# An MLP kernel in which the normalised rows of two token blocks are transposed by VectorE and placed by DMAs instead of by TensorE through PSUM

## The chip, the cores and the metric

One core of one Trainium2 chip. The metric is the device time of one execution in microseconds, the median of several runs. All numbers are of float32 data (TensorE works on float32 and on float32 split into a rounded part and a remainder).

## The reference, cut to what matters

A transformer block with adaptive normalisation, on 2048 tokens of width 576. An attention part (32 heads, one shared key and value head) is followed by an MLP of inner width 4608. What the change touches is the input of the MLP:

```python
h = _layernorm(x) * (1 + cb) + sb
y = _layernorm(h)
h = _gelu(y @ w1 + b1)
x = x + gb * (h @ w2 + b2)
```

For the product with `w1` the rows of `y` (token by feature) must lie transposed, with features on the partitions.

## The kernel before

**Tiling.** The 2048 tokens are four blocks of 512 (`NB`, `TB`), each of four tiles of 128 tokens (`NT`). The MLP takes the blocks in two pairs: the first pass handles blocks 0 and 1, the second blocks 2 and 3. In each pass there are 18 rounds (`NG`), one for each group of 256 inner features; so `v` counts 36 rounds, 0 to 35. Both matrix products use a scheme with seven products in place of eight (`A11`, `S2`, `S3`, `A12`, `S1`, `A22`, `S4`), for which sums of blocks of the operand are formed beforehand.

**A round.** The loop (from L1359) emits for each of the seven products the product with `w1` (`product`, L1156), the load of the same weights for the next round (`load_w1`, L792, on SyncE's queue), work of VectorE and ScalarE on the result (`gelu`, L1159 to L1177), and one step of the second matrix product of the round before (`fc2s`, L1247; its matmuls are L1259). Each step of `fc2s` uses both buffers of the PSUM tile `psA` (two tiles), and VectorE empties them in L1265. A step cannot start before VectorE has emptied the buffers of the step before. Each step then has its own weights for the next round loaded (`load_w2s`, L1223, SyncE's queue). The operands of `fc2s` are sums that GpSimd makes (`sums`, L1225 to L1245, with L1232 and L1233).

The step of `fc2s` between the two halves of product `S2` (the hook `mid`, L1397) is the seventh of the step list; the one right after `S2` is the first of the next list. They are called the seventh step and the first step below.

**Slots.** After each of the seven products the loop calls `more` (L1366). These seven calls of a round are called slots 1 to 7 here. In rounds 1 to 16 a slot advances the generator `ln2_pair` (L701) by one step, and this generator prepares the normalised rows of blocks 2 and 3, tile by tile, beside the MLP of blocks 0 and 1. Where the coming step contains a transposition it is marked `"T"`, and then only slots 3 and 4 (`room=True`) may run it; in round 16 (`NG - 2`) any slot may. In round 17 (`NG - 1`) whatever is left of the generator is run at once, and `op_pieces` (L1051) begins to form the operands of the second pass from `YR[1]`.

**The stages of a tile** are numbered steps (`ln2_stages`, L658). Stage 0 takes the statistics of the row on VectorE (L143, L670, L671), stage 1 turns them into scale and bias on GpSimd (L675 to L677), stage 4 normalises on ScalarE into a tile `Z` (L683), stage 5 applies scale and shift on GpSimd (L686, L687), stages 8 and 9 repeat the statistics and scale for the result, and stage 12 normalises again on ScalarE (L690, L691) and adds a bias row on GpSimd (L692). Stages 14 and 15 transpose: four and one TensorE transpositions of 128 by 128 into a PSUM tile (L155), each followed by a ScalarE copy into `yr` (L165). Tile i's stage k is put at step 10 i + k:

```python
return {0: lambda: stats(0), 1: lambda: scale(0), 4: norm, 5: rows, 8: lambda: stats(1), 9: lambda: scale(1),
        12: renorm, 14: lambda: turn(0, 4, ac), 15: lambda: turn(4, 5, ac)}
```

After the eighth tile the generator has two operations of GpSimd on `YR[1]`, one after the other (L714, L716); their result is what the operand `T2` of the second pass is copied from. In round 17, slot 2 forms `T2` (ScalarE L1069, named `+T2`), slot 3 its remainder (`-T2`, VectorE L1071) and the difference `=T3` (VectorE L1062), and only then comes the step of the second matrix product `fc2` (L1282; matmuls L1293, emptied by VectorE L1330), which uses the two `psA` buffers as well.

**The buffers.** `Z` is the tile `Z2`, with two buffers that are taken in turn. After the last tile the same two buffers receive weights (`load_w2`, L1135 to L1141).

**Queues.** Every engine works through its instructions in the order in which the program emits them. All DMAs of this part are issued by SyncE, in that order; one that has to wait holds up those behind it.

Of the kernel before, what the change touches and what calls it, by code (L numbers as in the profile page):

```python
# [8 lines left out]
F32 = mybir.dt.float32  # L9
# [9 lines left out]
KD = 5  # L19
# [13 lines left out]
def block_kernel(ctx: ExitStack, tc, x, wqkv, wo, w1, b1, w2, b2, c, wmod, ident_in, out):  # L33
    nc = tc.nc
    ve, ac, po, pe, sy = nc.vector, nc.scalar, nc.gpsimd, nc.tensor, nc.sync
# [17 lines left out]
    def psB(): return PS["t"].tile([128, 512], F32, name="psB", bufs=PS["b"])  # L53
# [27 lines left out]
    at = tc.tile_pool(name="at", bufs=1, side="right")  # L81
# [59 lines left out]
    def ln_stats1(src):  # L141
        stt = per.tile([128, 2, 6], F32, name="bst", bufs=3)
        ve.bn_stats(stt[:, 0, :], src[:, :288])  # L143
        return stt
# [9 lines left out]
    def tr(o, Z, k):  # L154
        pe.transpose(o, Z[:, 128 * k:128 * (k + 1)], ident)  # L155

    def transpose_tile(Z, yr, t, k0, k1, e):
        p = psB()
        for k in range(k0, k1):
            tr(p[:, 128 * (k - k0):128 * (k - k0 + 1)], Z, k)  # L160
        n = k1 - k0
        src = p[:, :128 * n].rearrange("p (k c) -> p k c", k=n)
        dst = yr[:, k0:k1, 128 * t:128 * (t + 1)]
        if e is ac:
            ac.activation(dst, src, AF.Copy)  # L165
        else:
            ve.tensor_copy(dst, src)
# [286 lines left out]
    for tb in range(NB):  # L454
        nz = big() if tb + 1 < NB else None
        for i, m in enumerate((4, 0, 1, 2, 3)):
# [27 lines left out]
            if tb < 2:  # L484
                for _ in range(NSTAT[tb][i]):
                    ln1_stats(*stats.popleft())
                for _ in range(NAPPLY[tb][i]):
                    b, t = applies.popleft()
# [8 lines left out]
    px = pxp.__enter__()  # L497
# [160 lines left out]
    def ln2_stages(tb, t):  # L658

        X = XT[:, NT * tb + t, :]  # L660
        o = {}

        def small(n):
            return per.tile([128, n], F32, name="sm2", bufs=8)

        def stats(i):
            src = o["h"] if i else X
            o["mv", i] = small(2)
            stt = ln_stats1(src)
            ve.bn_stats(stt[:, 1, :], src[:, 288:])  # L670
            ve.bn_aggr(o["mv", i], stt)  # L671

        def scale(i):
            mv, rs, nb = o["mv", i], small(1), small(1)
            po.tensor_scalar(rs, mv[:, 1:2], EPS, None, op0=ALU.add)  # L675
            po.tensor_tensor(rs, rs, nhalf, op=ALU.pow)
            po.tensor_scalar(nb, mv[:, 0:1], rs, -1.0, op0=ALU.mult, op1=ALU.mult)  # L677
            o["sc", i] = dict(scale=rs, bias=nb)

        def norm():  # L680
            Z = o["Z"] = px.tile([128, 640], F32, name="Z2", bufs=2)
            o["h"] = Z[:, :D]
            ac.activation(o["h"], X, AF.Identity, **o["sc", 0])  # L683

        def rows():
            po.tensor_mul(o["h"], o["h"], BC[:, 1, :])  # L686
            po.tensor_tensor(o["h"], o["h"], BC[:, 0, :], op=ALU.add)  # L687

        def renorm():
            ac.activation(o["Z"][:, D:], o["Z"][:, 512:D], AF.Identity, **o["sc", 1])  # L690
            ac.activation(o["h"], o["h"], AF.Identity, **o["sc", 1])  # L691
            po.tensor_tensor(X, X, B2["b"], op=ALU.add)  # L692

        def turn(k0, k1, e):
            yr = YR[tb // 2][:, KD * (tb % 2):KD * (tb % 2 + 1)]
            transpose_tile(o["Z"], yr, t, k0, k1, e)

        return {0: lambda: stats(0), 1: lambda: scale(0), 4: norm, 5: rows, 8: lambda: stats(1), 9: lambda: scale(1),
                12: renorm, 14: lambda: turn(0, 4, ac), 15: lambda: turn(4, 5, ac)}

    def ln2_pair():  # L701
        YR[1] = per.tile([128, 2 * KD, TB], F32, name="yr", tag="big", bufs=3)
        at = {}
        for _ in range(2):
            yield
        for i in range(2 * NT):
            for k, f in ln2_stages(2 + i // NT, i % NT).items():
                at.setdefault(10 * i + k, []).append((k >= 14, f))
        for k in range(max(at) + 1):
            for _, f in at.get(k, ()):  # L710
                f()
            yield "T" if any(t for t, _ in at.get(k + 1, ())) else None
        R = YR[1]
        po.tensor_tensor(R[:, 5:7], R[:, 7:9], R[:, 5:7], op=ALU.subtract)  # L714
        yield
        po.tensor_tensor(R[:, 5:7], R[:, 5:7], R[:, 0:2], op=ALU.add)  # L716
        yield
# [274 lines left out]
    for n in range(NQT):  # L992
# [8 lines left out]
        for tok in order:  # L1001
            if tok[0] == "V":
                g = int(tok[1:])
                while g:
                    i = min(g, 4 - pq % 4)
# [16 lines left out]
            elif tok == "WP":  # L1022
                h2 = part.popleft()
                p = psB()
# [81 lines left out]
    px = ctx.enter_context(tc.tile_pool(name="mx", bufs=1, side="right", reuse_waits="tile"))  # L1106
# [175 lines left out]
    def fc2(v):  # L1282
# [22 lines left out]
        for bt in range(2 * NT):  # L1305
# [30 lines left out]
            yield  # L1336

    fill = deque([ln2_pair()])
    f2 = deque()
    gens, sm = deque(), deque()  # L1340
# [175 lines left out]
```

## Time and profile before

| | |
|---|---|
| runs | 2221.74, 2223.95, 2224.66 us; median 2223.95 us |
| the profiled execution | 2222.87 us, of which 2221.0 us are the span from the first to the last instruction |
| busy in the span | TensorE 99%, its weight loads 65%, VectorE 87%, ScalarE 74%, GpSimd 69% |
| DMA | 307.71 MB in 184632 packets, mean 139 GB/s |
| granted TensorE clock | 0.999 of full speed over the span |
| the first pass of the MLP, rounds 0 to 17 | from 1388.0 to 1793.7 us of the span |

A row of a timeline gives the start (us from the span's start), the duration in us, the engine, the line of the kernel, the operation, what it writes and reads, the shape and how many are merged in the row; in brackets, the idle time of the engine just before and what ended it. PE is TensorE, PEld its weight loads, DVE VectorE, ACT ScalarE, POOL GpSimd, SPq the queue of SyncE.

### The profile page before, as it was taken

Reading aid. Unit: us, or ns where it says so; the run is one execution under the profiler, and the core shown is the slowest. Engines: PE = TensorE matmul, PEld = TensorE weight load, DVE = VectorE, ACT = ScalarE, POOL = GpSimd, SP = SyncE. Lnnn points to the kernel's source line nnn. Section 1 sums busy time; section 2 is a strip of 40 time slices with the busy share of each in tenths; the row PEclk is TensorE's granted clock in tenths of the full one; section 3 lists DMA queues with packets and bytes.
Section 4 is the critical chain, followed back from the end, with each engine's and each line's share of the span. In section 5 each row is a group of like instructions: output and inputs, shape, how many; then the busy total and the mean of one; then the engine's idle time right before and its main releaser. Section 6 shows DMA issues by size and latency. Waiting matters only on the chain.

```text
span 2221.0 us, 46122 instructions
## 1 busy us (share of the span) xinstructions
PE 2201.4 (99%) x16643; PEld 1449.3 (65%) x16643; DVE 1932.7 (87%) x3415; ACT 1639.2 (74%) x3144; POOL 1526.4 (69%) x1762
## 2 busy tenths in 40 slices
PE   8999999999999999999999999999999999999999
PEld 5654444444544545444454446888888899889898
DVE  7689999999999999999999983888888878788887
ACT  5569999999999999999999998544445444343443
POOL 7654455666776687678676540888888867877776
PEclk9999999999999999999999999999999999999999
DMA  6242143443333332333333321666666646676663
GB/s 228 86 133 92 34 134 117 135 129 116 126 119 118 115 130 97 112 130 111 117 127 117 120 70 63 207 178 175 179 179 180 184 128 182 180 219 189 178 183 123
DMA packets 184632, 307.71 MB, mean 139 GB/s; under 512 B 19695, under 2 KB 75391, under 8 KB 184405
## 3 DMA queue, kind: packets, MB, share of 16 engines
q1 hardware_dynamic: 184261, 304.62, 43.9%
q8 instruction: 132, 2.16, 0.4%
q14 instruction: 95, 0.78, 0.1%
q10 hardware_dynamic: 144, 0.15, 0.0%
HBM read 200.68 MB, written 93.79 MB: 133 GB/s over the span
## 4 chain that ended last, share of the span: by engine, by line
PE 93%; DVE 1%; ACT 1%; issue 0%; ACTq 0%; DVEq 0%
PE psC L932 24%; PE psB L1156 18%; PE psA L1259 16%; PE psB L942 14%; PE psM L319 13%; PE psB L731 2%; PE psB L952 2%; PE psA L1293 1%; PE psA L731 1%; PE psB L155 0%; PE psB L248 0%; PE psB L357 0%; PE psM L942 0%; ACT P L944 0%; DVE mx L344 0%; DVE gs L1168 0%
## 5 line engine op out<-in xcount | busy, mean ns | idle before, releaser
L944 ACT ACTIVATE P<-psB 128x512 f32<-128x512 f32 x2013 | 1054.4, 619 | 42.3 <-PE psM L319 20.6
L964 DVE TENSOR_REDUCE mx<-psM 128x1 f32<-128x512 f32 x1476 | 934.3, 682 | 28.5 <-PE psM L319 15.6
L942 PE MATMUL psB<-qst,KS 64*128 64x512 f32 x2013 | 605.1, 433 | 0.1
L319 PE MATMUL psM<-KS,qst 64*128 64x512 f32 x1722 | 590.2, 434 | 0.7 <-DVE mx L337 0.2
L932 PE MATMUL psC<-P,V 128*32 128x256 f32 (+3 forms) x6608 | 568.1, 439 | 0.0
L942 PEld LDWEIGHTS psB<-qst,KS 64*128 64x128 f32 x2013 | 301.7, 184 | 218.6 <-ACT P L944 186.2
L319 PEld LDWEIGHTS psM<-KS,qst 64*128 64x128 f32 x1722 | 283.5, 184 | 185.6 <-DVE mx L964 130.3
L1156 PE MATMUL psB<-ops,w1a 128*128 128x512 f32 x1512 | 393.9, 396 | 0.2 <-DVE h L1171 0.2
L1156 PEld LDWEIGHTS psB<-ops,w1a 128*128 128x128 f32 x1512 | 270.1, 188 | 46.7 <-DVE h L1171 0.6
L932 PEld LDWEIGHTS psC<-P,V 128*32 128x32 f32 x6608 | 147.0, 108 | 187.7 <-issue 160.2
L1265 DVE TENSOR_TENSOR XT<-psA,XT 128x576 f32<-128x576 f32 x330 | 241.8, 753 | 18.6 <-PE psA L1259 13.2
L1259 PEld LDWEIGHTS psA<-w2s,big 128*128 128x128 f32 x1584 | 223.0, 188 | 14.0 <-POOL big L1233 2.5
L1259 PE MATMUL psA<-w2s,big 128*128 128x288 f32 x1584 | 230.5, 294 | 0.0
L1169 ACT ACTIVATE psB<-gs 128x512 f32<-128x512 f32 x144 | 86.7, 602 | 127.6 <-DVE gs L1168 127.4
L1233 POOL TENSOR_TENSOR big<-s,big 128x512 fp32r<-128x512 f32 x132 | 171.0, 1295 | 10.6
L962 DVE CUSTOM_DVE_ANT_0 xc<-psM,xc 128x512 f32<-128x512 f32 x246 | 166.3, 682 | 12.9 <-PE psM L319 4.4
L1165 ACT ACTIVATE h<-psB,b1t 128x512 f32<-128x512 f32 x144 | 98.1, 681 | 100.7 <-PE psB L1156 76.7
L768 POOL TENSOR_TENSOR os<-O,os 128x512 fp32r<-128x512 f32 x31 | 39.8, 1285 | 171.8 <-ACT os L767 171.8
L955 ACT ACTIVATE xc<-psB 128x512 f32<-128x512 f32 x246 | 154.1, 626 | 3.0 <-PE psM L319 0.2
L1168 DVE SCALAR_TENSOR_TENSOR gs<-psB,h 128x512 f32<-128x512 f32 x144 | 98.6, 684 | 38.5 <-ACT psB L1166 38.4
L802 POOL TENSOR_TENSOR r<-r,r 128x256 fp32r<-128x256 f32 (+1 forms) x162 | 121.8, 752 | 13.0
L1174 ACT ACTIVATE big<-h 128x512 fp32r<-128x512 f32 x39 | 24.7, 634 | 133.8 <-DVE h L1171 133.8
(217 smaller groups left out, 3327.5 us busy)
## 6 DMA issues: line engine op xcount, KB each, us to landing
w1a<-w1scr SPq DMA_DIRECT2D x252, 256.0 KB
w2s<-w2sum SPq DMA_DIRECT2D x132, 288.0 KB
w1scr<-r SPq DMA_DIRECT2D x126, 256.0 KB
w2s<-w2scr SPq DMA_DIRECT2D x76, 288.0 KB
w2scr<-r SPq DMA_DIRECT2D x72, 288.0 KB
w2sum<-r SPq DMA_DIRECT2D x72, 288.0 KB
qst<-qscr SPq DMA_DIRECT2D x192, 72.0 KB
w1a<-w2scr SPq DMA_DIRECT2D x33, 288.0 KB
```

Source lines behind the costliest of these rows:

```text
L319: pe.matmul(o, QST[n][64 * g:64 * g + 64, p, 128 * qt:128 * (qt + 1)], KS[64 * g:64 * g + 64, 512 * kb:512 * (kb + 1)], start=True, stop=True)
L802: po.tensor_tensor(o[:, n:2 * n], src, o[:, :n].bitcast(F32), op=ALU.subtract)
L932: pe.matmul(PVt[n][32 * j:32 * (j + 1), cs], V[:, kc, :], t[:, j, cs], start=(kc == 0 and h0 == 0), stop=(kc == 15), skip_group_check=True)
L942: pe.matmul(t, KS[64 * g:64 * g + 64, 128 * kc:128 * (kc + 1)], QST[n][64 * g:64 * g + 64, i, :], start=True, stop=True)
L944: ac.activation(P[n, kc][:, 2 * i + g, :], t, AF.Exp, scale=SCALE)
L955: ac.activation(XC[-1], t, AF.Relu)
L962: ve.tensor_tensor_reduce(c, t, c, 1.0, -3.0e38, ALU.add, ALU.max, o)
L964: ve.tensor_reduce(o, t, axis=AX.X, op=ALU.max)
L1156: pe.matmul(o, x, y, start=(first and i == 0), stop=(i == len(terms) - 1), skip_group_check=True)
L1233: po.tensor_tensor(unit(u, 1), x, unit(u, 0).bitcast(F32), op=ALU.subtract)
L1259: pe.matmul(p[:, i, :288], x[:, ts_], W2S[k][:, y], start=(bool(first) and q == 0), stop=(q == 2), skip_group_check=True)
L1265: ve.tensor_tensor(o, p[:, :, :288], o, op=ALU.add)
```

## The change

The two transposition stages go. Stage 13 transposes the whole tile of 128 by 640 on VectorE, in blocks of 32 by 32 that stay where they are, into a second `Z2` buffer `T`. Stage 14 places the blocks by 16 DMAs on SyncE's queue: each takes 32 partitions and moves 5 by 32 pieces of 32 elements (128 bytes), 20 KB. Tile i's stage k is now put at step 9 i + k, and only the VectorE stage (13) is marked for slots 3 and 4.

```diff
-        def turn(k0, k1, e):
+        def turn():
+            o["T"] = px.tile([128, 640], F32, name="Z2", bufs=2)
+            ve.transpose(o["T"], o["Z"])
+
+        def spread():
             yr = YR[tb // 2][:, KD * (tb % 2):KD * (tb % 2 + 1)]
-            transpose_tile(o["Z"], yr, t, k0, k1, e)
+            for p in range(0, 128, 32):
+                for q in range(0, 128, 32):
+                    sy.dma_start(yr[q:q + 32, :, 128 * t + p:128 * t + p + 32],
+                                 o["T"][p:p + 32].rearrange("f (k c) -> f k c", k=KD)[:, :, q:q + 32])
 
         return {0: lambda: stats(0), 1: lambda: scale(0), 4: norm, 5: rows, 8: lambda: stats(1), 9: lambda: scale(1),
-                12: renorm, 14: lambda: turn(0, 4, ac), 15: lambda: turn(4, 5, ac)}
+                12: renorm, 13: turn, 14: spread}
...
         for i in range(2 * NT):
             for k, f in ln2_stages(2 + i // NT, i % NT).items():
-                at.setdefault(10 * i + k, []).append((k >= 14, f))
+                at.setdefault(9 * i + k, []).append((k == 13, f))
```

## Rows read from the trace of the kernel before

**Rows 1.** The page's chain that ended last: shares of the span by engine.

```profile
PE 93%; DVE 1%; ACT 1%; issue 0%; ACTq 0%; DVEq 0%
```

**Rows 2.** Timeline of ScalarE: the copy that opens a round (5, 6, 7; two of pass 2).

```profile
1489.27 0.60 ACT L1392 ACTIVATE u<-psB 128x512 f32<-128x512 f32 x1 [0.19 <-PE psB L1156]
...
1512.59 0.60 ACT L1392 ACTIVATE u<-psB 128x512 f32<-128x512 f32 x1
...
1535.57 0.60 ACT L1392 ACTIVATE u<-psB 128x512 f32<-128x512 f32 x1 [0.18 <-PE psB L1156]
...
1884.91 0.60 ACT L1392 ACTIVATE u<-psB 128x512 f32<-128x512 f32 x1 [0.17 <-PE psB L1156]
...
1907.68 0.60 ACT L1392 ACTIVATE u<-psB 128x512 f32<-128x512 f32 x1 [0.18 <-PE psB L1156]
```

**Rows 3.** Groups by line and form after 1360 us: busy us, mean ns | idle before.

```profile
L155 PE MATMUL psB<-ident,Z 128*128 128x128 f32 x40 | 7.0, 272 | 0.0
...
L165 ACT ACTIVATE yr<-psB 128x512 f32<-128x512 f32 x8 | 4.7, 582 | 0.0
```

**Rows 4.** VectorE's transposition in the attention part: ns min/median/max, first and last start us.

```profile
L749 DVE STREAM_TRANSPOSE T<-O x32: 700/702/711, 174.6 to 1372.9; 128x512 f32<-128x512 f32 x32
```

**Rows 5.** Timeline of VectorE: round 5 behind slot 3, then around the start of round 6.

```profile
1500.04 1.58 DVE L1265 TENSOR_TENSOR eb<-psA,eb 128x576 f32<-128x576 f32 x2 [2.00 <-PE psA L1259]
...
1513.12 0.45 DVE L143 BATCH_NORM_STATS2 bst<-Z 128x6 f32<-128x288 f32 x1
...
1514.10 0.64 DVE L1168 SCALAR_TENSOR_TENSOR gs<-psB,h 128x512 f32<-128x512 f32 x1
1514.65 1.41 DVE L1265 TENSOR_TENSOR XT<-psA,XT 128x576 f32<-128x576 f32 x2
```

**Rows 6.** Timelines of weight loads and GpSimd: first fc2s step, rounds 5 and 6.

```profile
1491.82 1.73 PEld L1259 LDWEIGHTS psA<-w2s,big 128*128 128x128 f32 x12
...
1515.47 1.62 PEld L1259 LDWEIGHTS psA<-w2s,big 128*128 128x128 f32 x12 [0.36 <-POOL big L1233]
...
1490.65 1.30 POOL L1233 TENSOR_TENSOR big<-s,big 128x512 fp32r<-128x512 f32 x1
...
1514.01 1.29 POOL L1233 TENSOR_TENSOR big<-s,big 128x512 fp32r<-128x512 f32 x1
```

**Rows 7.** Timeline of SyncE's queue: small transfers issued one behind another.

```profile
605.46 3.38 SPq L772 DMA_DIRECT2D big<-os  x4
...
206.89 2.46 SPq L315 DMA_DIRECT2D qst<-qscr  x6
...
177.42 0.52 SPq L538 DMA_DIRECT2D rowscr<-bc  x1
179.03 0.33 SPq L540 DMA_DIRECT2D gab<-rowscr  x1
```

**Rows 8.** SyncE's queue behind product A12, round 5; a load's use (weight loads, round 6).

```profile
1498.67 0.32 SPq L792 DMA_DIRECT2D w1a<-w1scr  x1
...
1500.85 0.52 SPq L1223 DMA_DIRECT2D w2s<-w2scr  x1
...
1521.77 1.37 PEld L1259 LDWEIGHTS psA<-w2s,gt 128*128 128x128 f32 x9
```

**Rows 9.** Timelines of SyncE, GpSimd, ScalarE, VectorE, weight loads: end of round 16, round 17.

```profile
1760.25 4.68 SPq L792 DMA_DIRECT2D w1a<-w1scr  x3
...
1768.37 2.41 POOL L714 TENSOR_TENSOR yr<-yr 128x1024 f32<-128x1024 f32 x1
...
1773.29 1.06 ACT L1069 ACTIVATE ops<-yr 128x1024 fp32r<-128x1024 f32 x1 [0.58 <-POOL yr L716]
...
1774.86 1.72 DVE L1071 TENSOR_TENSOR ops<-yr,ops 128x1024 fp32r<-128x1024 f32 x1
...
1777.64 1.41 DVE L1330 TENSOR_TENSOR XT<-psA,XT 128x576 f32<-128x576 f32 x2
...
1778.57 0.55 PEld L1293 LDWEIGHTS psA<-w2s,gt 128*128 128x128 f32 x3
```

## The prediction

> **What bounds the kernel now.** I read the chain of waits first: TensorE holds 93% of it and no engine's wait more than 1% [rows 1]. Whatever the change does counts by TensorE's time per round, so the next view is the row that opens a round. Round 5, which contains a tile's TensorE transpositions, takes 1512.59 - 1489.27 = 23.32 us; round 6, without them, 22.98 us; a round of the second pass, with the same matrix products and no row preparation, 22.77 us [rows 2]. So a turned tile costs up to 0.55 us, and round 6 loses 0.21 us to something else. The pattern repeats: seven turned tiles in the odd rounds 3 to 15, the eighth in round 16.
>
> Where does round 6 lose? Its first fc2s step starts after 0.36 us of idle time, put down to GpSimd's L1233 [rows 6]. I read it differently. In round 5 the same step started at 1491.82 though its L1233 ended only at 1491.95, so that isn't what the first weight load waits for [rows 6]. What both rounds share is the buffer rule: the step needs the `psA` buffer that VectorE empties for the seventh step. In round 6 VectorE first ran the second statistics of a tile (1513.12 to 1514.10), then a gelu operation, and began the emptying (1.41 us for two) at 1514.65; TensorE followed 0.82 us later, when the first of the two was done [rows 5, 6]. **VectorE at the head of an even round is therefore on the path.**
>
> **What goes.** Eight times five transpositions on TensorE (7.0 us busy, but overlapping) and two ScalarE copies each, the larger 582 ns [rows 3]. ScalarE sets no end here, so the copies count nothing. For TensorE I take 23.32 - 22.77 = 0.55 us for each of 8 tiles [rows 2]: **-4.4 us**. From below it is 23.32 - 22.98 = 0.34 us, 2.7 in all, from above 4.4 plus 7 times 0.21 us, 5.9 in all.
>
> **VectorE's transposition.** 128x512 takes 702 ns [rows 4]; by width 128x640 is about 0.88 us, an estimate. In odd rounds it stands at slot 3, and behind it VectorE idles 2.00 us before its next PSUM work [rows 5], so it is hidden; without that cover it would cost 8 x 0.88 = 7 us. It brings a wait: `T` takes the other `Z2` buffer, so the next tile's ScalarE normalisation, emitted in the same step, waits for the transposition. Behind it on ScalarE is the next gelu, which waits for product A12 anyway. VectorE in turn waits for the placing of the tile before, two rounds back.
>
> **The stage that moves.** Both versions need 14 slots, two rounds, per tile, because the marked step waits for slot 3. But by 9 i + k the first statistics of tile i+2 share a step with the second scale of tile i+1: 9(i+2) = 9(i+1) + 9. Counted from slot 3 of an odd round (step 9 i + 13), step 9 i + 18 is slot 1 of the even round. Before, 10(i+2) was six steps behind 10 i + 14 and fell into slot 2. Slot 1 is emitted ahead of the emptying of the seventh step. So in rounds 4, 6, ... 14 (tiles 2 to 7, six times) both sets of statistics stand before it. Like set for like set, that is 1514.10 - 1513.12 = 0.98 us more [rows 5], and TensorE, already waiting there, waits all of it: 6 x 0.98 = **+5.9 us**. Bounds: nothing, if L1233 is what holds the step; 6.6 us at 1.10 us a set (its three durations added are about that). GpSimd's scale operations move a slot too, ahead of sums that are needed some 10 us later: nothing.
>
> **The placing.** Sixteen transfers per tile, 128 in all, go into SyncE's queue. No row shows such a transfer. Nearest are those between SBUF and SBUF: four of L772 in 3.38 us, 0.85 us each. From HBM the issue is cheaper: six of L315 in 2.46 us, 0.41 each [rows 7]. I take 0.85, since source, target and second dimension agree. A landing I take from the write at 177.42 whose reader was issued at 179.03: 1.61 us [rows 7]. So a tile holds the queue for 16 x 0.85 = 13.6 us.
>
> In odd rounds that begins at slot 4, behind the load at 1498.67 in round 5 [rows 8], so about 1499. Behind it stand weight loads. The first frees at 1500.85 and is needed at 1521.77 [rows 8]; it would be issued at 1512.6 and land near 1514.2, so about 7 us of cover remain. That cover breaks beyond (1521.77 - 1.61 - 1499) / 16 = 1.32 us each. The bytes, 2.6 MB, are small beside 308 MB.
>
> The Trainium skill, "DMA: Bandwidth & Descriptors", Anatomy of one DMA, gives a fixed cost of about 2.0 us a transfer (stated for GpSimd's path), an estimate of 33 us for 16 in turn. The four transfers in 3.38 us don't pay it in turn [rows 7].
>
> **At the end there is no cover.** The eighth tile is turned at slot 5 of round 16 and placed at slot 6, behind the weight load issued at 1760.25 [rows 9]: from 1760.65 on, the last issue 15 x 0.85 later at 1773.4, landed at 1775.0. GpSimd's L714, emitted next, must wait for all of it. Before, it began at 1768.37; now 6.6 us later. Behind it follow, each in order: L716, ScalarE's `+T2` 4.92 us after L714 (1773.29, where ScalarE already waited for L716), 1.06 us long; VectorE's `-T2` and `=T3`, 2.78 us (1774.86 to 1777.64); then the first emptying, and 0.82 us behind its start the third step of `fc2`. Before, the emptying began at 1777.64, so the buffer came free near 1778.46, and that step started at 1778.57: no slack [rows 9]. New: 1775.0 + 4.92 + 1.06 + 2.78 + 0.82 = 1784.6, against 1778.57 - 0.55 = 1778.02 without the transpositions. **+6.6 us.** Bounds: at 0.41 us each the last lands at 1768.4, which costs 0.5 us; at 1.32 each it is 13.7 us. SyncE's loads behind it are used a round later, and the two `Z2` buffers for the last weights wait for the placing too, needed in round 18.
>
> **Sum:** -4.4 + 5.9 + 6.6 = +8.1 us against the profiled execution's 2222.87 us: **2231 us**. That execution is 1.08 us below the median shown, 2223.95. About 0.2%, 4.4 us, is what a measurement can tell from no change.
>
> **Rivals.**
> - *L1233 holds the first step (not slower).* If the profile's name for the 0.36 us is right, VectorE has slack there up to the end of L1233, and the moved statistics cost nothing until they pass it. Then -4.4 + 6.6 = +2.2, 2225 us. For it: L1233 ended at 1515.30, near the start at 1515.47; against it: round 5. 0.13.
> - *The placing is cheap.* At 0.41 us an issue the end is covered: -4.4 + 5.9 + 0.5 = +2.0, 2225 us. For it L315; against it, L772, which like the placing stays within SBUF, costs twice that. 0.14.
> - *Both:* -4.4 + 0.5 = -3.9, 2219 us, and 2217.5 if the 0.21 us of the even rounds goes too. 0.06.
> - *The transfers go one after another.* At 1.61 us each, L714 is 18.1 us late, and in seven odd rounds the queue ends at 1524.8, its first load landing at 1526.4 for 1521.77, 4.6 us late, 32 us: -4.4 + 5.9 + 18.1 + 32 = +52, 2275 us. Four in 3.38 us speak against it; pieces of 128 bytes that no row shows speak for it. 0.08.
>
> By the fixed cost that the Trainium skill gives in "DMA: Bandwidth & Descriptors" (Anatomy of one DMA), paid in turn, it would be this last case and worse.
>
> **How the numbers follow.** The forecast has 0.59. Slower by over 0.2%: 0.57 of it, 0.08, and 0.02 of the single cases: 0.67. Faster: 0.06 at most, from the third rival, whose 3.9 us lie at the bound; I give 0.05. Same: 0.28. The range reaches down to 2223, below both single cases (0.86 with the forecast), and up to 2243: the issue at 1.32 us (+7.1), statistics at 6.6 (+0.7) and the low gain (+1.7) together give 2241, and the median may lie a microsecond higher. The forecast's own range is 2227 to 2241.
>
> **What the profile will show.** Right: no L155 after 1400 us; odd rounds near 22.8 us, rounds 4 to 14 near 24.0, the first fc2s step idle some 1.3 us; L714 waiting for a DMA, and round 17 some 6 us longer. Wrong: even rounds unchanged, placing issues near 0.4 us, or, the other way, product or fc2s steps that wait for weights.

## The result, and the profile after

The changed kernel takes 2226.98 us (median; 2225.85 to 2229.3, 19 runs), the kernel before 2222.59 us beside it (2221.32 to 2224.66, 19 runs): ratio 1.0019, 95% interval 1.0013 to 1.0026. It is slower, by about 4.4 us, where 8.1 had been forecast. The profiled execution took 2225.85 us, 3.0 us above that of before; its MLP began 1.1 us earlier (first ScalarE copy at 1386.9 us of the span instead of 1388.0), so that the part from there on grew by 4.1 us.

Nearly all of it happens in rounds 2 to 17. The table gives round lengths, from one ScalarE copy that opens a round (L1392; L1399 after) to the next, in the profiled executions. The lower rows are the experiments below.

| kernel | odd, 5 to 15 (mean) | even, 4 to 14 (mean) | 16 | 17 | 2 to 17 together |
|---|---|---|---|---|---|
| before | 23.33 | 22.99 | 24.08 | 25.46 | 373.82 |
| **after** | 22.77 | 23.85 | 24.01 | 28.39 | 377.80 |
| e4 before, statistics in slot 1 | 23.33 | 23.90 | 24.08 | 25.47 | 379.29 |
| e1 after, statistics in slot 2 | 22.77 | 22.92 | 23.99 | 28.38 | 372.18 |
| e2 after, eighth tile on TensorE | 22.77 | 23.85 | 25.39 | 25.71 | 376.51 |
| e3 both | 22.77 | 22.92 | 25.38 | 25.71 | 370.97 |
| e7 both, eighth tile a slot later | 22.77 | 22.92 | 24.00 | 25.47 | 369.30 |
| e8 as e7, second statistics moved | 22.94 | 22.77 | 24.01 | 25.47 | 369.93 |

Odd rounds lose 0.55 us (unrounded lengths), even rounds gain 0.86, round 17 gains 2.93. The copy that opens round 17 comes straight behind other work of ScalarE, so rounds 16 and 17 are best read together. The page after gives TensorE's busy time and the chain that ended last, which answers to [rows 1]: GpSimd and DMA, absent before, now have a share of 1% each, VectorE 2% instead of 1%.

```profile
PE 2197.3 (99%) x16603; PEld 1445.2 (65%) x16603; DVE 1936.5 (87%) x3423; ACT 1634.1 (73%) x3128; POOL 1528.6 (69%) x1762
...
PE 94%; DVE 2%; ACT 1%; issue 1%; POOL 1%; DMA 1%; SPq 0%; DVEq 0%; ACTq 0%; POOLq 0%
```

The timeline of ScalarE, the copies that open rounds 5, 6 and 7 (answers to [rows 2]): 22.77 and 23.84 us, where 23.32 and 22.98 stood.

```profile
1488.34 0.60 ACT L1399 ACTIVATE u<-psB 128x512 f32<-128x512 f32 x1 [0.19 <-PE psB L1163]
...
1511.11 0.60 ACT L1399 ACTIVATE u<-psB 128x512 f32<-128x512 f32 x1 [0.17 <-PE psB L1163]
...
1534.95 0.60 ACT L1399 ACTIVATE u<-psB 128x512 f32<-128x512 f32 x1 [0.19 <-PE psB L1163]
```

**The head of an even round** (answers to [rows 5] and [rows 6]): timelines of weight loads, GpSimd and VectorE after, the first fc2s step of rounds 5 and 6.

```profile
1490.89 1.73 PEld L1266 LDWEIGHTS psA<-w2s,big 128*128 128x128 f32 x12
...
1514.85 1.61 PEld L1266 LDWEIGHTS psA<-w2s,big 128*128 128x128 f32 x12 [1.22 <-issue]
...
1512.46 1.31 POOL L1240 TENSOR_TENSOR big<-s,big 128x512 fp32r<-128x512 f32 x1
...
1511.58 0.45 DVE L143 BATCH_NORM_STATS2 bst<-Z 128x6 f32<-128x288 f32 x1
...
1513.10 0.45 DVE L143 BATCH_NORM_STATS2 bst<-XT 128x6 f32<-128x288 f32 x1
...
1514.07 1.37 DVE L1272 TENSOR_TENSOR XT<-psA,XT 128x576 f32<-128x576 f32 x2
```

VectorE now runs two sets of statistics, of `Z` and, from 1513.10, of `XT`, before it empties `psA`. Half of the pair of emptyings, 0.69 us, is over at 1514.76; TensorE goes on at 1514.85. GpSimd's L1240 had ended at 1513.77, 1.08 us earlier. So it was the buffer and not GpSimd. The view of waits groups it; TensorE's weight loads from 1460 to 1760 us, first the kernel before, then after (us in total, times, longest):

```profile
PEld psA L1259 <- POOL big L1233: 2.5, 7, 0.4
```

```profile
PEld psA L1266 <- issue: 7.4, 6, 1.2
PEld psA L1266 <- POOL big L1240: 0.3, 1, 0.3
```

**The end.** Timelines after of SyncE's queue, GpSimd, ScalarE, VectorE and weight loads, the end of round 16 and round 17 (answers to [rows 9]).

```profile
1760.66 10.39 SPq L702 DMA_DIRECT2D yr<-Z  x16
1771.15 1.01 SPq L799 DMA_DIRECT2D w1a<-w1scr  x2
...
1772.37 2.56 POOL L721 TENSOR_TENSOR yr<-yr 128x1024 f32<-128x1024 f32 x1 [3.82 <-DMA yr<-Z]
...
1777.42 1.06 ACT L1076 ACTIVATE ops<-yr 128x1024 fp32r<-128x1024 f32 x1 [5.20 <-POOL yr L723]
...
1780.79 1.41 DVE L1337 TENSOR_TENSOR XT<-psA,XT 128x576 f32<-128x576 f32 x2
...
1776.02 0.30 PEld L1163 LDWEIGHTS psB<-opt,w1a 128*128 128x128 f32 x2 [1.94 <-DMA w1a<-w1scr]
...
1781.59 0.43 PEld L1300 LDWEIGHTS psA<-w2s,gt 128*128 128x128 f32 x3 [1.81 <-DVE XT L1337]
```

TensorE idles twice: 1.94 us for a weight load that stands behind the placing in SyncE's queue, then 1.81 us for the chain L721, L723, L1076, L1078, L1069, L1337 that the last placing transfer releases.

**VectorE's transposition and the placing in the middle** (answers to [rows 4], [rows 5] and [rows 8]). The transposition and the placing by their lines (ns min/median/max, first and last start in us):

```profile
L696 DVE STREAM_TRANSPOSE Z<-Z x8: 833/835/846, 1448.3 to 1758.5; 128x640 f32<-128x640 f32 x8
...
L702 SPq DMA_DIRECT2D yr<-Z x128: 594/602/1712, 1451.6 to 1770.4; - x128
```

The timelines of VectorE and of SyncE's queue in round 5:

```profile
1494.90 0.83 DVE L696 STREAM_TRANSPOSE Z<-Z 128x640 f32<-128x640 f32 x1
...
1498.57 1.56 DVE L1272 TENSOR_TENSOR eb<-psA,eb 128x576 f32<-128x576 f32 x2 [1.52 <-PE psA L1266]
...
1497.82 10.41 SPq L702 DMA_DIRECT2D yr<-Z  x16
1508.33 0.58 SPq L1230 DMA_DIRECT2D w2s<-w2scr  x1
```

VectorE still idles 1.52 us behind the transposition (2.00 before): it is hidden. Sixteen transfers hold the queue for 10.4 us, 0.65 us from one to the next.

### The profile page after: what moved, and what is told of

Read it like the earlier page. It is cut to its first block, busy times and chain, and to the rows that moved or that the text cites. A ratio compares the mean times of both kernels' runs of the same rounds, so it can differ in the third digit from the quotient of the medians.

```text
span 2224.1 us, 46209 instructions
## 1 busy us (share of the span) xinstructions
PE 2197.3 (99%) x16603; PEld 1445.2 (65%) x16603; DVE 1936.5 (87%) x3423; ACT 1634.1 (73%) x3128; POOL 1528.6 (69%) x1762
## 4 chain that ended last, share of the span: by engine, by line
PE 94%; DVE 2%; ACT 1%; issue 1%; POOL 1%; DMA 1%; SPq 0%; DVEq 0%; ACTq 0%; POOLq 0%
PE psC L939 24%; PE psB L1163 18%; PE psA L1266 16%; PE psB L949 14%; PE psM L319 13%; PE psB L738 2%; PE psB L248 2%; PE psB L959 2%; PE psA L1300 1%; PE psA L319 1%; PE psA L738 1%; DMA bigw<-in_wmod 0%; PE psB L155 0%; SPq L702 0%; DVE mx L344 0%
## 5 line engine op out<-in xcount | busy, mean ns | idle before, releaser
L1240 POOL TENSOR_TENSOR big<-s,big 128x512 fp32r<-128x512 f32 x132 | 171.2, 1297 | 10.6
L969 DVE CUSTOM_DVE_ANT_0 xc<-psM,xc 128x512 f32<-128x512 f32 x246 | 166.2, 682 | 12.9 <-PE psB L949 6.0
```

The lines of the kernel that those rows point to most:

```text
L969: ve.tensor_tensor_reduce(c, t, c, 1.0, -3.0e38, ALU.add, ALU.max, o)
L1240: po.tensor_tensor(unit(u, 1), x, unit(u, 0).bitcast(F32), op=ALU.subtract)
```

## The experiments

Theory: three terms of the forecast, each with its place: TensorE's saved transpositions (odd rounds and the eighth tile), statistics on VectorE's path (even rounds), the eighth tile's rows (round 17). Rivals: GpSimd holds the first step; the placing itself costs in the middle; round 17 is a matter of the weight load alone.

**e1: the statistics back in slot 2.** In the changed kernel, stages 0 and 1 of tiles 2 to 7 one step later:

```diff
-                at.setdefault(9 * i + k, []).append((k == 13, f))
+                at.setdefault(9 * i + k + (k < 2 and i > 1), []).append((k == 13, f))
```

> The changed kernel with one part undone: from the third tile on, the first statistics and their scale go one step later, so that VectorE's statistics stand in slot 2 of the even round again, as before the change. Theory (the moved statistics delay the emptying of the seventh step's PSUM buffers): rounds 4, 6, ... 14 fall from 23.85 to about 22.98 us, six times 0.87, so 5.2 us less: about 2221.8 us. Rival (GpSimd's L1233 holds the first step, or the cost is VectorE's transposition itself): even rounds stay at 23.85, about 2227.0 us.

Measured: 2222.45 us (2220.19 to 2224.48), ratio to the kernel before 0.9995 [0.9986, 1.0004]; even rounds 22.92. TensorE's wait at the first step, 1.22 us, is 0.30 now, as the timeline of weight loads in round 6 shows:

```profile
1516.23 1.61 PEld L1266 LDWEIGHTS psA<-w2s,big 128*128 128x128 f32 x12 [0.30 <-POOL big L1240]
```

So the moved statistics are worth 6 x (23.85 - 22.92) = 5.6 us by the rounds and 4.9 by the medians, each taken against the kernel before that ran beside it.

**e4: that one move alone, in the kernel before.**

```diff
-                at.setdefault(10 * i + k, []).append((k >= 14, f))
+                at.setdefault(10 * i + k - (k < 2 and i > 1), []).append((k >= 14, f))
```

> The kernel before, with TensorE's transpositions, and one part of the change alone: from the third tile on, the first statistics and their scale go one step earlier, into slot 1 of the even round. Theory: rounds 4, 6, ... 14 rise from 22.98 to about 23.85 us, 5.2 us more than the kernel before: 2227.8 us. Rival (the statistics cost only together with VectorE's transposition): no change, 2222.6 us.

Measured: 2228.69 us (2227.29 to 2229.75), ratio 1.0022 [1.0013, 1.0031]; even rounds 23.90, odd ones and the end as before. By weight loads of round 6 the first step waits 1.28 us, put down, as in the changed kernel, to "issue":

```profile
1518.11 1.61 PEld L1259 LDWEIGHTS psA<-w2s,big 128*128 128x128 f32 x12 [1.28 <-issue]
```

The same loss without a placing DMA or a transposition on VectorE: 6 x (23.90 - 22.99) = 5.5 us. What slowed the even rounds is the order of stages and no part of the new transposition. Both edits move GpSimd's scale operations along with the statistics; that it is VectorE's part is read from the rows above (GpSimd done 1.08 us before the step) and from e8.

**e2: the eighth tile as before.** In the changed kernel that tile alone goes through TensorE, PSUM and ScalarE again:

```diff
+        if (tb, t) == (NB - 1, NT - 1):
+            yr7 = YR[1][:, KD:]
+            return {0: lambda: stats(0), 1: lambda: scale(0), 4: norm, 5: rows, 8: lambda: stats(1), 9: lambda: scale(1),
+                    12: renorm, 13: lambda: transpose_tile(o["Z"], yr7, t, 0, 4, ac),
+                    14: lambda: transpose_tile(o["Z"], yr7, t, 4, 5, ac)}
```

> The changed kernel with the eighth tile alone transposed by TensorE and copied by ScalarE as before; seven tiles keep the placing by DMAs. Theory (the end has no cover: the last placing delays GpSimd's L714 and the weight loads behind it in SyncE's queue): round 17 falls from 28.4 to about 25.5 us, TensorE pays about 0.5 us for the five transpositions, so about 3 us less: 2224.0 us. Rival (the cost of the placing is spread over all tiles, by traffic or by the queue): an eighth of it at most goes, and round 17 stays above 28: about 2226.7 us.

Measured: 2225.87 us (2224.45 to 2227.1), ratio 1.0012 [1.0003, 1.002]. Round 17 fell to 25.71 us as expected, but round 16 rose by 1.38, so that 1.3 us came in these rounds where 3 had been expected. The timeline of weight loads shows why: with steps 13 and 14 the transposition stands in slot 5, one slot ahead of its place in the kernel before, and waits for its PSUM buffer until VectorE's L1183 (a gelu operation) is done.

```profile
1758.96 0.42 PEld L155 LDWEIGHTS psB<-ident,Z 128*128 128x128 f32 x4 [1.82 <-DVE h L1183]
```

**e3: e1 and e2 together.**

> Both of the above at once. Theory (the two costs are independent, since one is in the even rounds 4 to 14 and one in round 17): 5.2 and 3.0 us less, about 2218.8 us, which is below the kernel before by about 3.8 us, the gain of seven tiles without TensorE transpositions. Rival (a wait taken away comes back at the next one): 2221 us or more.

Measured: 2220.07 us (2218.77 to 2223.88), ratio 0.9988 [0.9979, 0.9997]. By the rounds the two effects add; 1.3 us are left in round 16.

**e7: e3 with the eighth tile's transpositions in slots 6 and 7** (steps 14 and 15 in place of 13 and 14).

```diff
-                    12: renorm, 13: lambda: transpose_tile(o["Z"], yr7, t, 0, 4, ac),
-                    14: lambda: transpose_tile(o["Z"], yr7, t, 4, 5, ac)}
+                    12: renorm, 14: lambda: transpose_tile(o["Z"], yr7, t, 0, 4, ac),
+                    15: lambda: transpose_tile(o["Z"], yr7, t, 4, 5, ac)}
```

> Both edits of the kernel that took 2220.07 us (first statistics in slot 2, the eighth tile turned by TensorE and ScalarE), but that tile's two transpositions stand one slot later, in slots 6 and 7 of round 16, where the kernel before had them. Theory: in slot 5 TensorE stood 1.82 us in front of the transposition (its PSUM buffer was freed by VectorE's L1183) and round 16 came to 25.38 us instead of 24.0; one slot later that wait goes, round 17 stays at 25.7 or less, and the tail is that of the kernel before: what is left of the change is seven tiles without TensorE, 7 x 0.55 = 3.9 us below the kernel before, about 2218.7 us (2218.0 to 2219.3). Rival: the wait is the price of the eighth tile on TensorE wherever it stands; then 2220.1 us and round 16 stays at 25.4 us.

Measured: **2218.69 us** (2217.3 to 2220.19, 11 runs) against 2223.2, ratio 0.9979 [0.997, 0.9988]: 4.5 us faster than the kernel before and the lowest median of all (e8 cannot be told from it). Rounds 16 and 17 are those of the kernel before. What is left is seven tiles without TensorE, 7 x 0.55 = 3.9 us, and 0.6 us in rounds 2 and 4 to 14.

**e8: does VectorE or GpSimd hold the last 0.3 us of even rounds?** As e7, but the second statistics leave slot 7 of the odd round, where they run ahead of the emptying (the first statistics, the scales and the second normalisation move to later slots with them).

```diff
+        def slot(i, k):
+            if i == 0:
+                return k + (k > 12)
+            return 14 * i + {0: -6, 1: -5, 4: 0, 5: 1, 8: 6, 9: 7, 12: 10, 13: 14, 14: 15}[k] - (2 if i == 7 and 5 < k < 13 else 4 if i == 7 and k > 12 else 0)
...
-                at.setdefault(9 * i + k + (k < 2 and i > 1), []).append((k == 13, f))
+                at.setdefault(slot(i, k), []).append((False, f))
```

> As the kernel with the eighth tile one slot later, and the second statistics of tiles 2 to 7 stand in slots 2 and 3 of the even round instead of slot 7 of the odd one and slot 1 of the even one (the first statistics go to slots 4 and 5, the second normalisation to slot 6). Theory: VectorE, late by the second statistics in slot 7, holds the first step of fc2s by its additions L1272 (in the kernel with both edits the first of the pair ended at about 1514.4 us, the step began at 1514.55 us after 0.30 us idle); without them even rounds fall from 22.92 to 22.77 us, six or seven of them, 0.9 to 1.0 us less, about 2217.7 us. Rival, from the prediction: GpSimd's halves of the sums (L1240, ended 1514.40 us) hold that step; then even rounds stay at 22.9 us and the time stays at 2218.7 us.

Measured: 2219.09 us (2217.51 to 2221.32), ratio 0.998 [0.9971, 0.9989]: no gain over e7. Yet even rounds fell to 22.77, and the view of waits shows none at all for TensorE's weight loads from 1460 to 1735 us. The timelines of GpSimd and weight loads, round 6:

```profile
1511.94 1.29 POOL L1251 TENSOR_TENSOR big<-s,big 128x512 fp32r<-128x512 f32 x1
...
1513.13 1.73 PEld L1277 LDWEIGHTS psA<-w2s,big 128*128 128x128 f32 x12
```

GpSimd's operation (L1251 here) ends 2.65 us after the round's opening copy, as in e7, and the step starts 0.10 us before that end: it was VectorE, not GpSimd. But odd rounds rose by 0.17 and round 2 by 0.52. No wait in the records explains the 0.17; that stays open.

**e11: are the two waits of round 17 two costs or one?** In the changed kernel the load that causes the first wait goes out from ScalarE's queue:

```diff
-            sy.dma_start(W1["r"][:, a:b].bitcast(F32), w1scr[i, :, a:b])
+            e = ac if w == "tails" and v == NG - 2 else sy
+            e.dma_start(W1["r"][:, a:b].bitcast(F32), w1scr[i, :, a:b])
```

> The changed kernel, in which the one load of the tails' weights that round 17 uses is issued from ScalarE's queue and so does not stand behind the eighth tile's placing. TensorE idles twice in round 17: 1.94 us for that load, then 1.81 us for the chain that starts with the eighth tile's last transfer (GpSimd L721, L723, ScalarE L1076, VectorE L1078, L1337). Theory: the chain alone sets when TensorE goes on (1781.6 us); without the first wait TensorE comes 1.9 us earlier to the second and waits 3.7 us there; the time stays at 2227.0 us (2226.5 to 2227.5). Rival: the two waits add up; then 1.9 us less, 2225.1 us.

Measured: 2228.58 us (2226.85 to 2230.82) against 2223.2, ratio 1.0021 [1.0012, 1.003]: nothing gained, and above the expected 2226.5 to 2227.5. The first wait is gone, the second has grown from 1.81 to 3.61 us, and TensorE goes on at 1781.52 us instead of 1781.59. The chain from the last placing transfer alone sets when TensorE goes on. Yet round 17 is longer, 29.71 us for 28.39. The timeline of weight loads of e11, then its stretches (us, PE busy, granted clock, DMA share, GB/s):

```profile
1781.52 0.74 PEld L1301 LDWEIGHTS psA<-w2s,gt 128*128 128x128 f32 x3 [3.61 <-DVE XT L1338]
1782.17 0.81 PEld L1301 LDWEIGHTS psA<-w2s,big 128*128 128x128 f32 x3
```

```profile
1778.00:1782.00 4.00, 0.82 (x4) 0.88 0.92 332
1782.00:1784.00 2.00, 2.00 (x10) 0.50 0.05 18
```

The same of the changed kernel:

```profile
1781.97 0.46 PEld L1300 LDWEIGHTS psA<-w2s,big 128*128 128x128 f32 x3
```

```profile
1779.00:1782.00 3.00, 1.62 (x9) 1.00 1.03 378
1782.00:1784.00 2.00, 2.00 (x15) 1.00 0.39 146
```

Joined to one stretch, the same idle time costs more: behind 3.61 us without work the granted clock is 0.50, the lower level, 1.2 GHz, and three weight loads take 0.81 us instead of 0.46. In the changed kernel the two waits are kept apart by work of TensorE, and the clock stays at 1.00.

**e6: the placing doubled.** Each transfer is split in two; the same bytes and packets in 32 transfers per tile.

```diff
-                    sy.dma_start(yr[q:q + 32, :, 128 * t + p:128 * t + p + 32],
-                                 o["T"][p:p + 32].rearrange("f (k c) -> f k c", k=KD)[:, :, q:q + 32])
+                    for ks in (slice(0, 3), slice(3, KD)):
+                        sy.dma_start(yr[q:q + 32, ks, 128 * t + p:128 * t + p + 32],
+                                     o["T"][p:p + 32].rearrange("f (k c) -> f k c", k=KD)[:, ks, q:q + 32])
```

> The changed kernel with each placing transfer split in two (blocks 0 to 2 and 3 to 4 of the features), 32 transfers per tile in place of 16, the same bytes and the same packets. Theory: a transfer costs SyncE's queue 0.65 us whatever it carries; the queue is held 20.8 us per tile instead of 10.4, the eighth tile's rows land 10.4 us later and round 17 is that much longer; in the middle the loads behind the placing go out 10.4 us later, and of these the tails' (asked at 1511.89, landed 1517.61, used at 1520.69 us: 3.1 us of cover) come some 7 us late in each even round, seven times: 2227.0 + 10.4 + 7 x 7 = about 2286 us (2265 to 2295). Rival 1, the prediction's own bound (loads behind the placing are used a round later, their cover lasts to 1.32 us per transfer of 16, 0.66 of 32): only the tail, about 2237 us. Rival 2: the price goes with the packets; then the queue is held 10.4 us as before and the time stays at 2227 us.

Measured: 2301.59 us (2299.57 to 2302.87), ratio 1.0347 [1.0332, 1.0363]; even rounds 32.84, round 17 39.48. Both rivals fall: the price goes with the transfer, and in the middle cover was short. The weight load that first breaks is the tails'; it costs TensorE 51.1 us in seven even rounds, 7.3 each (10.4 - 3.1 of cover). The view of waits, once from 1440 to 1850 us and once to 1900, so with round 17:

```profile
PEld psB L1164 <- DMA w1a<-w1scr: 51.1, 7, 7.8
...
PEld psB L1164 <- DMA w1a<-w1scr: 63.0, 8, 11.9
```

Timelines of weight loads (the second of these waits) and of SyncE's queue (the last tile's placing, the larger part of it), then the stretches around that wait:

```profile
1537.89 0.50 PEld L1164 LDWEIGHTS psB<-opt,w1a 128*128 128x128 f32 x2 [7.05 <-DMA w1a<-w1scr]
...
1787.15 13.32 SPq L703 DMA_DIRECT2D yr<-Z  x20
```

```profile
1531.00:1538.00 7.00, 0.39 (x3) 0.70 0.96 334
1538.00:1540.00 2.00, 2.00 (x7) 0.50 1.05 379
1540.00:1542.00 2.00, 2.00 (x10) 0.50 1.03 394
1542.00:1544.00 2.00, 2.00 (x6) 0.50 0.46 117
1544.00:1546.00 2.00, 2.00 (x14) 0.98 0.51 153
```

It came 15 us above the estimate and 7 above its range, and nearly all of that lies in the seven rounds: they grew by 9.0 us each where 7 was expected, 7.3 of it the wait. The rest fits what stands behind the wait: in the stretch shown the clock was 0.50 from 1538 to 1544 us. Round 17 grew by 39.48 - 28.39 = 11.1 us (10.4 expected).

**e12: the last placing on two queues.** e1, with eight of the eighth tile's sixteen transfers issued by ScalarE:

```diff
-                    sy.dma_start(yr[q:q + 32, :, 128 * t + p:128 * t + p + 32],
-                                 o["T"][p:p + 32].rearrange("f (k c) -> f k c", k=KD)[:, :, q:q + 32])
+                    e = ac if (tb, t) == (NB - 1, NT - 1) and p >= 64 else sy
+                    e.dma_start(yr[q:q + 32, :, 128 * t + p:128 * t + p + 32],
+                                o["T"][p:p + 32].rearrange("f (k c) -> f k c", k=KD)[:, :, q:q + 32])
```

> The kernel with the first statistics in slot 2 (2222.45 us), in which eight of the eighth tile's sixteen placing transfers go out from ScalarE's queue and eight from SyncE's; all eight tiles stay without TensorE. Theory: it is the issuing on one queue, 16 x 0.65 us, that made the last rows late; two queues have them landed about 5 us earlier (1767 instead of 1772 us), the tails' load goes out as much earlier, both waits of round 17 (1.94 and 1.81 us) go, and round 17 comes to 25.5 us from 28.4: about 2219.5 us (2219 to 2220.5). Against that stands what ScalarE loses: eight issues of 0.35 us (its one load of weights) to 0.65 us are 2.8 to 5.2 us in slot 6 of round 16, where each gelu of ScalarE's stands behind them. Rival: TensorE then waits for ScalarE as long as it had waited for the rows, and the time stays at 2222.5 us.

Measured: 2223.45 us (2221.77 to 2224.4), ratio 1.0 [0.9991, 1.0008]: the rival. The waits of round 17 shrink to 0.6 us, but ScalarE's own work stands behind its issues, and TensorE waits in round 16, 28.41 us long (ScalarE, then weight loads):

```profile
1759.46 5.51 ACTq L703 DMA_DIRECT2D yr<-Z  x8
1765.02 0.60 ACT L1177 ACTIVATE psB<-gs 128x512 f32<-128x512 f32 x1 [5.15 <-DMA w1a<-w1scr]
...
1767.08 2.11 PEld L1267 LDWEIGHTS psA<-w1a,big 128*128 128x128 f32 x12 [3.58 <-issue]
```

ScalarE's idle time is named after a weight load; in truth the engine was issuing. Nor did the rows come sooner, as the theory had it. SyncE's second load into `Z`, which has to wait for the placing, and GpSimd's L722, which reads the rows, both stand until 1769.0 us:

```profile
1764.99 4.20 SPq L1149 DMA_DIRECT2D Z<-w2scr  x2
...
1769.03 2.39 POOL L722 TENSOR_TENSOR yr<-yr 128x1024 f32<-128x1024 f32 x1 [0.66 <-DMA Z<-w2scr]
```

That is 4.1 us after ScalarE's last issue ended at 1764.97, and 12.9 us after the tile's first placing transfer (1756.10), where e1 with one queue needed 11.7.

**e13: the same with GpSimd** (`po` in place of `ac`).

> The same with GpSimd's queue in place of ScalarE's. Theory: as there, about 2219.5 us, if an issue costs GpSimd no more than SyncE (0.65 us): in slot 6 GpSimd has about 1.9 us of idle time per slot, so 5.2 us of issues set it back some 3 us, and L721 follows on GpSimd and waits for the rows anyway. Rival: an issue holds GpSimd for over 1.3 us; then the eight take as long as sixteen of SyncE's, GpSimd's low halves and sums come late as well, and the time is 2222.5 us or more.

Measured: 2225.44 us (2224.0 to 2227.15), ratio 1.0011 [1.0002, 1.002]. The issues cost no more than SyncE's, so the reason that I gave for the rival isn't what happened; its time is. GpSimd's timeline, then the weight load behind it:

```profile
1760.06 4.24 POOL L703 DMA_DIRECT2D yr<-Z  x7
1765.02 0.57 POOL L703 DMA_DIRECT2D yr<-Z  x1 [0.73 <-issue]
1765.61 1.32 POOL L1185 TENSOR_TENSOR big<-h,big 128x512 fp32r<-128x512 f32 x1
1769.76 2.40 POOL L722 TENSOR_TENSOR yr<-yr 128x1024 f32<-128x1024 f32 x1 [2.83 <-DMA yr<-Z]
...
1778.83 0.74 PEld L1301 LDWEIGHTS psA<-w2s,gt 128*128 128x128 f32 x3 [5.38 <-DVE XT L1338]
```

And the stretch behind that wait (columns as above):

```profile
1779.00:1782.00 3.00, 3.00 (x13) 0.50 0.00 0
```

The last issue ends at 1765.59, and the rows are there only at 1769.76, 4.2 us later (SyncE's in the changed kernel: 1.3 us after the end of the last issue, 1771.05 to 1772.37). From the first placing transfer (1756.10) it is 13.7 us. TensorE waits 5.38 us in one stretch, with the clock at the lower level behind it; round 17 takes 32.83 us. The Trainium skill, "Perfetto Trace Analysis" (DMA Instruction — SWDGE), says that such a row of GpSimd ends when the descriptors are made and not when the data have moved; the 4.2 us agree with that, but the 4.1 us behind ScalarE's issues in e12 are as long, so they show nothing that is GpSimd's own.

What e12 and e13 share is, first, that the second engine's issues start late, behind its other work (1759.46 and 1760.06), so that the last one ends only 1.5 and 0.9 us sooner after the first transfer than on one queue (10.4); and then that SyncE, with eight transfers fewer, sends weight loads while the placing is still under way: the DMA share from 1763 to 1767 us is 0.89 to 1.04 in these two, and 0.50 and 0.21 in the changed kernel. That those loads delay the small transfers is likely, but no run tests it by itself.

## Why the prediction was right, and where its size was off

The direction and all three mechanisms held; the sum was 8.1 us where some 4.4 came. The measured 2226.98 us lies at the lower edge of the forecast's own range (2227 to 2241), not much above the 2225 us of the rival with a cheap placing.

- **TensorE's saving, -4.4.** Right: odd rounds lost 0.55 us each, as forecast, and e7, which keeps seven of eight, lies 4.5 us below the kernel before, 3.9 of it in the odd rounds.
- **Which engine holds the first step.** Right: the rival that gave it to GpSimd falls by the changed kernel's own trace (GpSimd done 1.08 us before the step) and by e8, where the step starts before GpSimd's operation ends.
- **The moved statistics, +5.9.** Right: 5.6 us by e1, 5.5 by e4. Even rounds came to 23.85 us (24.0 forecast), the idle time to 1.22 us (1.3).
- **VectorE's transposition, 0.88 us and hidden.** 0.836 us, and hidden. ScalarE's next normalisation did wait for it, 6.6 us in seven times, and that cost nothing.
- **The eighth tile, +6.6. This is the mis-sized term.** The step that failed is the price of one issue, taken as 0.85 us from L772 [rows 7] because source and target agree; it was 0.65, between that row and L315's 0.41. The last issue came at 1770.45 instead of 1773.4; its landing took up to 1.92 us, 0.3 more than the 1.61 assumed. The rows arrived 2.6 us earlier than forecast (1772.37 for 1775.0), and the chain behind L721 took 9.22 us to TensorE (4.92 + 1.06 + 2.78 + 0.82 = 9.58 forecast). Measured: rounds 16 and 17 grew by 2.85 us together, which is 3.4 in the prediction's terms: it counted 0.55 us as saved there, and no run shows that saving by itself. The bound of 0.5 us at 0.41 us an issue does not come out of the prediction's own chain (1768.4 + 9.58 = 1778.0, nothing); the 18.1 us of its last rival are 18.0.
- **"SyncE's loads behind it are used a round later".** Wrong for the tails' load. It is issued behind the placing and already used in product A12 of the next round, so its cover in the middle is 3.1 us (landed at 1517.61, used at 1520.69 in the changed kernel), not the 7 of the load in [rows 8]. It also lands late, 5.7 us after its issue, among the loads that the placing held up; the limit had been worked out with 1.61. At 0.65 us an issue the cover held; the limit of 1.32 us per transfer was too wide, as e6 shows with twice as many. In round 17 it made a wait of 1.94 us that had not been forecast, but e11 shows that this wait hid behind the other.

With the measured terms: -4.4 + 5.6 + 3.4 = +4.6. Rounds 2 to 17 grew by 377.80 - 373.82 = 3.98 us; of the rest, 0.17 is in round 2, and 6 x (22.99 - 22.92) = 0.4 is what even rounds lose when the statistics stay where they were (e1); no run says why.

The fixed cost of 2.0 us a transfer of the Trainium skill ("DMA: Bandwidth & Descriptors", Anatomy of one DMA) is not paid in turn here: sixteen transfers held the queue for 10.4 us, where the estimate from it was 33. For one transfer by itself it is near the 1.92 us from the start of the last issue to its reader.

## What to carry to other kernels

When stages of a software pipeline are renumbered, work out for every stage, also for those that the change doesn't mean, into which slot it falls: here a pitch of 9 in place of 10 moved one stage by a slot and cost 5.6 us, more than the new transposition saved. Price a row of small DMAs by the queue time of one issue times their number, and look at both ends: the weight loads queued behind them, each with its own first use, and the last item of the loop, which has nothing left to hide behind. A step that pays in the middle can be left out for that last item (e7).

## What the runs showed of the hardware that was not expected

- Issuing is priced by the transfer: 0.65 us on SyncE's queue, with 160 pieces of 128 bytes as with 96 or 64 (e6: 20 in 13.32 us), 0.7 on ScalarE's (5.51 us for eight), and about 0.6 on GpSimd.
- Two queues did not bring the rows sooner: from the tile's first transfer to its reader it took 11.7 us on SyncE's queue alone (e1), 12.9 with ScalarE's (e12) and 13.7 with GpSimd's (e13), the last data 4.1 and 4.2 us after the end of the last issue instead of 1.3.
- Two waits of 1.94 and 1.81 us with work between them left TensorE's granted clock at 1.00; one of 3.6 us (e11), of 5.4 (e13) or of 7 (e6) was followed by 0.50, for some 2 us in e11 and some 6 in e6.
